# Separate value buffers refilled as soon as they are read, and one continuous sequence of row maxima

## The chip, the core and the metric

The kernel runs on one core of one Trainium2 chip. The metric is device time in microseconds (us). Five engines work side by side, each through its own instructions in a fixed order: PE (matrix products; its weight loads are listed as PEld), DVE (vector), ACT (activations), POOL (GpSimd) and SP, which here only issues DMAs. An instruction at the head of an engine's queue that waits holds up everything behind it.

## The reference

Attention over 8 batches and 8 heads, 1152 keys, 576 pooled queries, head size 64, followed by a gated unit:

```python
q_pool = q.reshape(B, H, S // factor, factor, D).mean(axis=3)
scores = scale * np.matmul(q_pool, k.transpose(0, 1, 3, 2))
scores = scores - np.max(scores, axis=-1, keepdims=True)
attn = np.exp(scores)
attn = attn / (np.sum(attn, axis=-1, keepdims=True) + 1e-09)
out = np.matmul(attn, v)                       # heads side by side: x, 8 x 576 x 512
h = np.maximum(x @ w_in, 0.0);  u, v = halves of h
v_n = normalised v;  v_s = w_spatial @ v_n + b_spatial
y = (u * v_s) @ w_out
```

## The kernel before

The work is cut into 32 pairs: two heads of one batch, four pairs to a batch. Every fp32 operand is split into a high and a low fp16 part (names ending in `hi`, `lo`) so that fp16 products give nearly fp32 accuracy. What happens to pair i, stage by stage:

- `load_kq(i)` fetches keys and queries into `kq` (one buffer, L222 and L223). `prep(i)` squares both for a scale (L132 on ACT), adds the two query rows that are pooled (L292 on POOL), splits into `xq`, `qhi`, `khi`, `klo` (L135, L302, L304 on ACT, L138 on DVE, L305 on POOL) and copies parts across partitions with DMAs (L299 to L313). There are three sets of these operands, so prep runs two pairs ahead.
- `norm_v(i)` fetches the values and squares them (L132) for a scale of the whole batch, four pairs ahead; `split_v(i)` fetches them again, scales and splits them into `vp` (L261, L262 on ACT, L264 on POOL), one pair ahead. Both fetch into `vt`, two buffers used in turn.
- `maxima(i)` finds the row maxima of the scores one pair ahead: 27 steps of a product of 384 columns (L342, or L333 for the mixed tile) into PSUM tile `pm` (or `pw` while no unit runs) and a reduction on DVE (L348). Then a last reduction `mx` (L352), a transpose (L356), a split into `mr` (L358, L359), and two small DMAs (L363) put the maxima into two extra rows of `xq`, so that the score product subtracts them.
- `attention(i)` has 18 score tiles: two products each (L506, L507) into one of three `pss` banks, the exponential on ACT (L512), every two tiles a split of the probabilities on POOL (L524), and four ticks later the products with the values (L428, L432, L435) into the single bank `o`; at the end of a head DVE normalises them into `xm` (L407, L408, L443). The 64 tail queries go the same way through `ptl` (L520, L524, L478 to L484).
- A unit of two batches (eight pairs) then runs as `gated_unit`, its steps mixed into the next eight pairs: DVE has much to do in the pairs 10, 18, 26 (normalising, L611 to L624) and 14, 22, 30 (a split, L138). The weights come as doubles and are turned into fp32 during the first eight pairs (`from_double`, L149 to L161, nearly all on DVE).

All of these are Python generators. `attention(i)` gives out 40 ticks, and after each tick the others advance by their rate (`Pace`: so many steps per tick, from a given tick on); at the end of a pair what is left is run out. That is the order of writing only. A scheduler beneath the language then sets the order on each engine: it goes by the order of writing, but where its own model of times holds an instruction not ready, it takes a later one that is. So an instruction may stand far ahead of where it was written, as far as its buffers allow; on the chip that order is fixed.

Of the kernel before, what the change touches and what calls it, by code (L numbers as in the profile page):

```python
# [12 lines left out]
F32 = mybir.dt.float32  # L13
# [18 lines left out]
def attn_sgu_kernel(ctx: ExitStack, tc: tile.TileContext, qT, kT, v, w_in, w_spT, b_sp, w_out, out):  # L32
    nc = tc.nc
    P = 128
    B, NHP, _, D, _, S = qT.shape
    NC = kT.shape[4]
    NP = B * NHP
# [20 lines left out]
    ld = ctx.enter_context(tc.tile_pool(name="ld", bufs=1))  # L58
# [66 lines left out]
    def scale_of(sq, name):  # L125
        tot = sm.tile([P, 1], F32, name=name + "t", bufs=2)
        nc.vector.reduce_sum(out=tot, in_=sq, axis=AX.X)
        yield
        return (yield from scales(tot, name))

    def square_sum(acc, src, junk):
        nc.scalar.activation(junk, src, AF.Square, bias=0.0, scale=1.0, accum_out=acc)  # L132
# [85 lines left out]
    def load_kq(i):  # L218

        b, hp = divmod(i, NHP)  # L220
        kq = ld.tile([P, 2 * KEYS], F32, name="kq")
        nc.sync.dma_start(out=kq[:, 0:KEYS], in_=kT[b, hp].rearrange("h d c p -> (h d) (c p)"))  # L222
        nc.sync.dma_start(out=kq[:, KEYS:], in_=qT[b, hp].rearrange("h d r s -> (h d) (r s)"))  # L223
        state[i] = {"kq": kq}

    def load_v(i):
        b, hp = divmod(i, NHP)
        vt = ld.tile([P, 2, NC, D], F32, name="vt", bufs=2)
        nc.sync.dma_start(
            out=vt.rearrange("p h c d -> p h (c d)"),  # L230
            in_=v[b, 2 * hp : 2 * hp + 2].rearrange("h (p c) d -> p h (c d)", c=NC),
        )
        return vt

    vsq = {}
    vscale = {}

    def norm_v(i):

        b, hp = divmod(i, NHP)  # L240
        if hp == 0:
            vsq[b] = sm.tile([P, 2 * NHP], F32, name="vsq", bufs=2)
        vt = load_v(i)
        yield
        yield
        for h in range(2):
            square_sum(vsq[b][:, 2 * hp + h : 2 * hp + h + 1], vt[:, h], vt[:, h])
            yield
        if hp == NHP - 1:
            vscale[b] = yield from scale_of(vsq.pop(b), "v")  # L250
            yield

    def split_v(i):

        vt = load_v(i)
        yield
        yield
        s_v = vscale[i // NHP][0]
        vp = vps[i % 2]
        for h in range(2):  # L260
            nc.scalar.activation(vt[:, h], vt[:, h], AF.Copy, bias=0.0, scale=s_v)  # L261
            nc.scalar.activation(vp[:, h, :, D : 2 * D], vt[:, h], AF.Copy, bias=0.0, scale=1.0)  # L262
            yield
            nc.gpsimd.tensor_sub(vp[:, h, :, 0:D], vt[:, h], vp[:, h, :, D : 2 * D])  # L264
            yield

    def values_ahead(i):
        if i + NHP < NP:
            yield from norm_v(i + NHP)
        if i + 1 < NP:  # L270
            yield from split_v(i + 1)

    def prep(i):
        st = state[i]
# [7 lines left out]
        for j in range(2):  # L282
            square_sum(sq[:, j : j + 1], kq[:, j * KEYS : (j + 1) * KEYS], KL[:, 0].rearrange("p c k -> p (c k)"))
            yield
        s, r = yield from scales(sq, "qk")
        esc = sm.tile([P, 1], F32, name="esc", bufs=NSET)
        nc.vector.scalar_tensor_tensor(
            out=esc, in0=r[:, 0:1], scalar=ESC, in1=r[:, 1:2], op0=ALU.mult, op1=ALU.mult
# [22 lines left out]
        nc.sync.dma_start(out=X[lower, 1], in_=X[upper, 0])  # L311
        nc.sync.dma_start(out=KL[lower, 1], in_=KL[upper, 0])
        nc.sync.dma_start(out=KL[D:KR, 0], in_=KL[D:KR, 1])  # L313
        yield


    def maxima(i):
        st = state[i]
# [52 lines left out]
    LAG = 4  # L371
    TAIL_SPLIT = 5
    TAIL_AT = 9
    PREP_AT = 3
    PREP_RATE = 0.35
    V_RATE = 0.35
    W_RATE = 0.25
    W_AT = 4
    MAX_RATE = 1.0

    units = []

# [6 lines left out]
    def ends_unit(i):  # L389
        return i % (2 * NHP) == 2 * NHP - 1  # L390
# [387 lines left out]
    def step(gen):  # L778
        return None if gen is None or next(gen, StopIteration) is StopIteration else gen
# [13 lines left out]
    def drain(gen):  # L793
        while gen is not None:
            gen = step(gen)

    load_kq(0)
    drain(norm_v(0))
    drain(prep(0))
    load_kq(1)  # L800
    for i in range(1, NHP):
        drain(norm_v(i))
    drain(maxima(0))
    drain(split_v(0))
    drain(prep(1))
    weights = load_weights()
    spatial_weights = [None]
    credit = 0.0
    for i in range(NP):
        if i + 2 < NP:  # L810
            load_kq(i + 2)
        run = [
            Pace(maxima(i + 1), MAX_RATE) if i + 1 < NP else None,
            Pace(values_ahead(i), V_RATE),
            Pace(prep(i + 2), PREP_RATE, PREP_AT) if i + 2 < NP else None,
            Pace(weights, W_RATE, W_AT if i == 0 else 0),
        ]
        for _ in attention(i):
            for r in run:
                if r:  # L820
                    r.tick()
            credit = min(credit + MOE_RATE, 2.0)
            while credit >= 1 and units:
                credit -= 1
                unit_step()
        for r in run[:3]:
            if r:
                drain(r.gen)
        weights = run[3].gen
        if ends_unit(i) and i < 2 * NHP:  # L830
            drain(weights)
            weights = None
            spatial_weights[0] = step(load_spatial())
# [49 lines left out]
```

## Time and profile before

| | |
|---|---|
| three runs | 1371.06, 1373.02, 1377.21 us; median 1373.02 |
| profiled execution | 1378.83 us, its span on the core 1377.1 us |
| granted PE clock, mean | 0.967 |
| busy share PE, DVE, ACT, POOL | 89%, 70%, 70%, 62% |
| DMA | 123.77 MB, mean 90 GB/s |
| chain that ended last | PE 47%, DVE 25%, ACT 8%, POOL 7%, DMA 7% |

In what follows a pair is taken to begin with the first of its 18 exponentials (L512). The first begins at 48.46 us, pair 8 at 328.6 us, the last pair (31) at 1236.7 us; what follows pair 31 is the last unit alone. A row of a group gives engine, line, tile names as out<-in and count, then busy us and mean ns of one, then the idle time of the engine just before and who ended it. A row of a wait gives who waited for whom, us in total, how often, and the longest. A row of a window gives its length, then busy us and count for each engine, the granted PE clock, the DMA share and GB/s.

### The profile page before, as it was taken

To read this page: it belongs to the slowest core of one execution; us is meant where nothing else is said; L and a number is where in the kernel's file an instruction comes from. 1 tells how busy PE (TensorE), PEld (TensorE's weight loads), DVE (VectorE), ACT (ScalarE), POOL (GpSimd) and SP (SyncE) were. 2 spreads that over 40 slices of the span, in tenths; PEclk is the share of its full clock that TensorE was granted. 3 is DMA by queue.
4 is the path that set the end of the run, shared out by engine and by line. 5 is a ranking of instruction groups with operands and counts; after the bars stand their busy time and mean duration, and the time that the engine had idled before them with its cause. 6 is when DMAs were issued, how large, how long until landed. Compare 5 with 4: busy or idle time off the path is not lost.

```text
span 1377.1 us, 33478 instructions
## 1 busy us (share of the span) xinstructions
PE 1222.1 (89%) x13696; PEld 741.5 (54%) x13696; DVE 967.1 (70%) x2068; ACT 970.6 (70%) x1632; POOL 847.0 (62%) x492
## 2 busy tenths in 40 slices
PE   3677887788998999889998999889998999899998
PEld 1354555555554665556555666555555566556443
DVE  5799889986869767765668766775667866761455
ACT  6777678779966777768776886768776776655333
POOL 3587677878755666657774766667666576655000
PEclk9998899989999999999999999999999999999999
DMA  7533343434333231244332132244331131101002
GB/s 252 166 97 109 94 124 94 128 93 139 113 96 96 79 94 56 62 126 135 96 96 87 51 91 84 74 118 135 104 96 42 47 94 55 28 24 40 8 1 69
DMA packets 56346, 123.77 MB, mean 90 GB/s; under 512 B 8256, under 2 KB 16448, under 8 KB 56192
## 3 DMA queue, kind: packets, MB, share of 16 engines
q1 hardware_dynamic: 56192, 121.63, 29.8%
q8 instruction: 107, 1.75, 0.5%
q14 instruction: 47, 0.39, 0.1%
HBM read 83.56 MB, written 9.44 MB: 68 GB/s over the span
## 4 chain that ended last, share of the span: by engine, by line
PE 47%; DVE 25%; ACT 8%; POOL 7%; DMA 7%; issue 4%; SPq 1%; POOLq 0%; ACTq 0%; DVEq 0%
DVE mt L348 7%; PE pss L507 5%; PE pss L506 5%; PE pw L688 5%; POOL pt L524 4%; PE pm L342 4%; PE pw L731 4%; PE pw L646 3%; PE o L435 3%; PE o L428 3%; PE pw L582 3%; ACT pt L512 3%; DMA kq<-in_qT_dram 3%; PE o L432 3%; DVE vv L138 2%
## 5 line engine op out<-in xcount | busy, mean ns | idle before, releaser
L524 POOL TENSOR_TENSOR pt<-pt 128x1024 f16<-128x1024 f32 x288 | 567.8, 1977 | 265.9 <-ACT pt L512 253.8
L512 ACT ACTIVATE pt<-pss,lnp,esc 128x512 f32<-128x512 f32 x576 | 439.4, 776 | 156.7 <-PE pss L507 148.1
L348 DVE TENSOR_REDUCE mt<-pm 128x1 f32<-128x384 f32 x730 | 395.8, 552 | 139.1 <-PE pm L342 119.2
L435 PE MATMUL o<-vp,pt 128*128 128x65 f16 x2304 | 282.8, 198 | 20.2 <-POOL pt L524 19.9
L428 PE MATMUL o<-vp,pt 128*128 128x65 f16 x2304 | 284.8, 196 | 13.0 <-DVE xm L443 12.8
L506 PE MATMUL pss<-qhi,khi 128*128 128x64 f16 (+1 forms) x1152 | 279.6, 294 | 9.1 <-ACT pt L512 8.0
L432 PE MATMUL o<-vp,pt 128*128 128x64 f16 x2304 | 284.5, 196 | 0.0
L507 PE MATMUL pss<-xq,klo 66*128 66x64 f16 (+1 forms) x1152 | 280.6, 295 | 4.1 <-DMA xq<-mr 4.1
L428 PEld LDWEIGHTS <-pt 128*128 128x128 bf16 x2304 | 222.7, 101 | 85.1 <-DVE xm L443 22.0
L432 PEld LDWEIGHTS <-pt 128*128 128x128 bf16 x2304 | 221.6, 100 | 50.7 <-issue 10.5
L342 PE MATMUL pm<-khi,qhi 128*128 128x384 f16 x652 | 217.9, 335 | 32.6 <-DVE mt L348 27.7
L435 PEld LDWEIGHTS <-pt 128*128 128x128 f16 x2304 | 220.7, 100 | 31.6 <-POOL pt L524 24.8
L507 PEld LDWEIGHTS <-klo 66*128 66x128 f16 x1152 | 99.1, 100 | 48.8 <-issue 17.3
L132 ACT ACTIVATE klo<-kq 128x1152 f16<-128x1152 f32 x64 | 74.6, 1166 | 63.7 <-DMA kq<-in_kT_dram 49.4
L506 PEld LDWEIGHTS <-khi 128*128 128x128 f16 x1152 | 103.5, 100 | 27.9 <-issue 12.2
L342 PEld LDWEIGHTS <-qhi 128*128 128x128 f16 x768 | 76.8, 101 | 66.3 <-issue 28.5
L524 POOL TENSOR_TENSOR ptl<-ptl 128x1152 f16<-128x1152 f32 x32 | 71.1, 2221 | 57.9 <-ACT ptl L520 57.9
L305 POOL TENSOR_TENSOR klo<-kq,khi 128x640 f16<-128x640 f32 x64 | 85.1, 1341 | 20.1 <-ACT khi L304 19.8
L520 ACT ACTIVATE ptl<-pss,lnp,esc 128x256 f32<-128x256 f32 (+1 forms) x128 | 75.6, 591 | 24.8 <-PE pss L507 24.2
L264 POOL TENSOR_TENSOR vp<-vt,vp 128x576 f16<-128x576 f32 x64 | 80.6, 1264 | 20.3 <-ACT vp L262 20.3
L582 PE MATMUL pw<-wi_h,xg 128*128 128x512 f16 x240 | 90.1, 382 | 0.0
L731 PE MATMUL pw<-wo_h,vv 128*128 128x512 f16 x216 | 80.3, 381 | 4.7 <-DVE vv L138 4.7
(177 smaller groups left out, 2394.2 us busy)
## 6 DMA issues: line engine op xcount, KB each, us to landing
vt<-in_v_dram SPq DMA_DIRECT2D x64, 576.0 KB
kq<-in_kT_dram SPq DMA_DIRECT2D x32, 576.0 KB
kq<-in_qT_dram SPq DMA_DIRECT2D x32, 576.0 KB
khi<-khi SPq DMA_DIRECT2D x96, 144.0 KB
out_dram<-row SPq DMA_DIRECT2D x24, 256.0 KB
qhi<-xq SPq DMA_DIRECT2D x64, 72.0 KB
klo<-klo SPq DMA_DIRECT2D x32, 144.0 KB
vv<-in_w_in_dram SPq DMA_DIRECT2D x8, 512.0 KB
```

Source lines behind the costliest of these rows:

```text
L305: nc.gpsimd.tensor_sub(KL[:, 0, a:z], k0[:, a:z], khh[:, 1, a:z])
L342: nc.tensor.matmul(pm[:, :W], lhsT=qhl[:, h, c0 : c0 + P], rhs=khh[:, h, n * NB : (n + 1) * NB, :], start=True, stop=True,)
L348: nc.vector.reduce_max(out=mt[:, t, n : n + 1], in_=pm[:, :W], axis=AX.X)
L428: nc.tensor.matmul(o[:, t], lhsT=top[:, cols], rhs=vp[:, D : D + D1], start=c == 0 and t == 0, stop=False, skip_group_check=True,)
L432: nc.tensor.matmul(o[:, t, 0:D], lhsT=top[:, cols], rhs=vp[:, 0:D], start=False, stop=False, skip_group_check=True)
L435: nc.tensor.matmul(o[:, t], lhsT=rst[:, cols], rhs=vp[:, D : D + D1], start=False, stop=c == NC - 1, skip_group_check=True,)
L506: nc.tensor.matmul(o, lhsT=khh[:, h, c, :], rhs=qhl[:, h, q], start=True, stop=False)
L507: nc.tensor.matmul(o, lhsT=KL[0:KR, h, c, :], rhs=X[0:KR, h, q], start=False, stop=True)
L512: nc.scalar.activation(pt, ps, AF.Exp, bias=lnp, scale=esc)
L524: nc.gpsimd.tensor_sub(t.bitcast(F16)[:, :, 0::2], t, t.bitcast(BF16)[:, :, 1::2])
L582: nc.tensor.matmul(ph, lhsT=xa[:, cc, c0 : c0 + P], rhs=wa[:, cc, DH:DF], start=n == 0, stop=n == 3 * NCC - 1,)
L731: nc.tensor.matmul(py, lhsT=ga[:, fc, c0 : c0 + P], rhs=wa[:, fc, :], start=m == 0, stop=m == end - 1)
```

## The change

Four things change.

1. The values get two buffers with names of their own: `vn` for `norm_v`, `vs` for `split_v` (one each, so the memory is the same). A fetch is written right behind the last read of its buffer: `norm_v(i)` ends with the fetch for the next one, `split_v(i)` with the fetch for `split_v(i + 1)`, and `prep(i)` ends with `load_kq(i + 1)`. Before, each was written where the data was wanted, with two idle steps behind it.
2. The maxima of the pairs 1 to 31 become one generator, `all_maxima`, which advances on all ticks at 0.85 steps per tick (before: one generator per pair, begun with pair i for pair i + 1, at 1.0). The maxima of a pair begin when those of the pair before are done and `prep` of the pair was finished at least four ticks ago (`LANDING`). What a pair must have is still run out before it.
3. `norm_v` and `split_v` are paced apart (0.4 from tick 0, and 0.3 from tick 16; before one after the other at 0.35), and `prep` begins at tick 2 in place of 3.
4. Before the first pair, `prep(0)` is written ahead of the four `norm_v`.

```diff
+    vts = {}
+    def load_v(i, name):
+        if i < NP:
+            b, hp = divmod(i, NHP)
+            vt = ld.tile([P, 2, NC, D], F32, name=name)
+            nc.sync.dma_start(...)
+            vts[i, name] = vt
...
-    def norm_v(i):
+    def norm_v(i, name="vn", ahead=1):
...
-        vt = load_v(i)
-        yield
-        yield
+        vt = vts.pop((i, name))
         for h in range(2):
             square_sum(vsq[b][:, 2 * hp + h : 2 * hp + h + 1], vt[:, h], vt[:, h])
             yield
+        load_v(i + ahead, name)
+        yield
...
     def split_v(i):
-        vt = load_v(i)
-        yield
-        yield
+        vt = vts.pop((i, "vs"))
...
             nc.gpsimd.tensor_sub(vp[:, h, :, 0:D], vt[:, h], vp[:, h, :, D : 2 * D])
             yield
-
-    def values_ahead(i):
-        if i + NHP < NP:
-            yield from norm_v(i + NHP)
-        if i + 1 < NP:
-            yield from split_v(i + 1)
+        load_v(i + 1, "vs")
+        yield
...
         nc.sync.dma_start(out=KL[D:KR, 0], in_=KL[D:KR, 1])
-        yield
-
+        if i + 1 < NP:
+            load_kq(i + 1)
+        prepped[i] = now[0] + LANDING
+        yield
+
+    prepped = {}
+    now = [0]
+    LANDING = 4
+    known = set()
+
+    def all_maxima():
+        for i in range(1, NP):
+            while prepped.get(i, 1 << 30) > now[0]:
+                yield
+            yield from maxima(i)
+            known.add(i)
...
-    PREP_AT = 3
+    PREP_AT = 2
     PREP_RATE = 0.35
-    V_RATE = 0.35
+    NORM_RATE = 0.4
+    V_RATE = 0.3
+    V_AT = 16
...
-    MAX_RATE = 1.0
+    MAX_RATE = 0.85
...
     load_kq(0)
-    drain(norm_v(0))
+    load_v(0, "vn")
+    load_v(1, "vs")
     drain(prep(0))
-    load_kq(1)
-    for i in range(1, NHP):
-        drain(norm_v(i))
+    drain(norm_v(0, "vn", 2))
+    drain(norm_v(1, "vs", 2))
+    drain(norm_v(2, "vn", 2))
+    drain(norm_v(3, "vs", -3))
     drain(maxima(0))
     drain(split_v(0))
     drain(prep(1))
     weights = load_weights()
+    maxima_pace = Pace(all_maxima(), MAX_RATE)
...
     for i in range(NP):
-        if i + 2 < NP:
-            load_kq(i + 2)
         run = [
-            Pace(maxima(i + 1), MAX_RATE) if i + 1 < NP else None,
-            Pace(values_ahead(i), V_RATE),
+            Pace(norm_v(i + NHP), NORM_RATE) if i + NHP < NP else None,
+            Pace(split_v(i + 1), V_RATE, V_AT) if i + 1 < NP else None,
             Pace(prep(i + 2), PREP_RATE, PREP_AT) if i + 2 < NP else None,
...
         for _ in attention(i):
-            for r in run:
+            now[0] += 1
+            for r in [maxima_pace, *run]:
...
         weights = run[3].gen
+        while i + 1 < NP and i + 1 not in known:
+            prepped[i + 1] = now[0]
+            maxima_pace.gen = step(maxima_pace.gen)
```

What the scheduler makes of it is seen on the engines. First DVE, from the end of pair 13 into pair 14, before the change (`mr` belongs to the maxima of pair 14, `row` and `u` to the unit; L348 are the first maxima of pair 15):

```order
L443 TENSOR_TENSOR xm<-o,den 128x4x64
L358 TENSOR_SCALAR mr<-pm 9x128
L359 SCALAR_TENSOR_TENSOR mr<-pm,mr 9x128
L695 SCALAR_TENSOR_TENSOR row<-pw,r_v,b_bc 128x512
L698 TENSOR_TENSOR u<-u,row 128x512
L695 SCALAR_TENSOR_TENSOR row<-pw,r_v,b_bc 128x64
L698 TENSOR_TENSOR u<-u,row 128x64
L635 TENSOR_SCALAR r_v<-wsr 128x1
L127 TENSOR_REDUCE gt<-gsq 128x1
L117 TENSOR_SCALAR gh<-pm 128x1
L121 TENSOR_SCALAR gs<-gh 128x1
L348 TENSOR_REDUCE mt<-pm 128x1
```

The same place with the change, where the lines have other numbers (L372 and L373 are L358 and L359, L459 is L443, L362 is L348, L711 and L714 are L695 and L698, L651 is L635):

```order
L373 SCALAR_TENSOR_TENSOR mr<-pm,mr 9x128
L459 TENSOR_TENSOR xm<-o,den 128x4x64
L362 TENSOR_REDUCE mt<-pm 128x1
L711 SCALAR_TENSOR_TENSOR row<-pw,r_v,b_bc 128x512
L362 TENSOR_REDUCE mt<-pm 128x1
L714 TENSOR_TENSOR u<-u,row 128x512
L362 TENSOR_REDUCE mt<-pm 128x1
L711 SCALAR_TENSOR_TENSOR row<-pw,r_v,b_bc 128x64
L362 TENSOR_REDUCE mt<-pm 128x1
L714 TENSOR_TENSOR u<-u,row 128x64
L362 TENSOR_REDUCE mt<-pm 128x1
L651 TENSOR_SCALAR r_v<-wsr 128x1
```

Five reductions of pair 15 now stand in the end of pair 13; before, none did, and the first came behind the start of the unit's split in pair 14. On PE the end of pair 13 (behind the transpose L356) holds five maxima products between the last score tiles, before none. So it is in the pairs 8 to 29, with five or six each, and in the pairs 1, 2 and 5; in the pairs 0, 3, 4, 6 and 7 the end of the pair still has none, or only its last moments.

Second SP, where the keys of pair 6 are fetched, before and then with the change (L222 and L223 fetch, `khi` and `klo` are the copies of prep; with the change L305, L306, L308 copy `khi`, L310 and L311 `klo`, L233 fetches values):

```order
L308 DMA khi_118<-khi_118 64x1152
L312 DMA klo_109<-klo_109 64x1152
L222 DMA kq<-in_kT_dram 128x1152
L363 DMA xq_114<-mr 1x9x128 x2
L310 DMA khi_118<-khi_118 64x1152
L313 DMA klo_109<-klo_109 2x1152
L223 DMA kq<-in_qT_dram 128x1152
```

```order
L306 DMA khi_118<-khi_118 64x1152
L310 DMA klo_109<-klo_109 64x1152
L222 DMA kq<-in_kT_dram 128x1152
L308 DMA khi_118<-khi_118 64x1152
L311 DMA klo_109<-klo_109 2x1152
L223 DMA kq<-in_qT_dram 128x1152
```

The fetch of keys and queries stands at the same place, behind the first copy of `klo`: it was there although it was written elsewhere. The DMAs of the maxima (L363) are no longer among these, here.

Third SP about the fetch for pair 12, before and then with the change (L299 and L297 begin the copies of the next prep):

```order
L313 DMA klo_109<-klo_109 2x1152
L223 DMA kq<-in_qT_dram 128x1152
L229 DMA vt<-in_v_dram 128x2x576
L363 DMA xq_114<-mr 1x9x128 x2
L229 DMA vt<-in_v_dram 128x2x576 x2
L299 DMA qhi_119<-xq_113 64x576
```

```order
L311 DMA klo_109<-klo_109 2x1152
L223 DMA kq<-in_qT_dram 128x1152
L233 DMA vn<-in_v_dram 128x2x576
L377 DMA xq_114<-mr 1x9x128 x2
L233 DMA vn<-in_v_dram 128x2x576 x3
L233 DMA vs<-in_v_dram 128x2x576
L297 DMA qhi_119<-xq_113 64x576
```

Three fetches into the one buffer `vn` stand in a row ahead of the next copies. With a buffer of its own the chain of `norm_v` runs ahead of its place: all its squares stand before pair 14, where before nearly every pair up to 25 had one.

More of the change, by code (lines that the diff above doesn't have):

```diff
@@ L224, in load_kq @@
         state[i] = {"kq": kq}
[L226 to L233, printed above, removed]
+    vts = {}
[3 more added lines that the diff above has]
+            vt = ld.tile([P, 2, NC, D], F32, name=name)
+            nc.sync.dma_start(
+                out=vt.rearrange("p h c d -> p h (c d)"),
+                in_=v[b, 2 * hp : 2 * hp + 2].rearrange("h (p c) d -> p h (c d)", c=NC),
+            )
+            vts[i, name] = vt
     vsq = {}
     vscale = {}
-    def norm_v(i):
+    def norm_v(i, name="vn", ahead=1):
         b, hp = divmod(i, NHP)
```

## The prediction

> **What bounds the kernel now.** I read first the span by stretch, cut where the exponentials of a pair begin: the start; pairs 0 to 7; pairs 8 to 30; pair 31 and the last unit.
>
> ```profile
> core 0: us, PE busy (x) PEld busy (x) DVE busy (x) ACT busy (x) POOL busy (x), PEclk, DMA share, GB/s
> 0.00:48.46 48.46, 16.31 (x51) 5.90 (x52) 27.96 (x65) 30.91 (x61) 17.12 (x22) 1.00 0.71 226
> 48.46:328.60 280.14, 224.58 (x2803) 147.37 (x2803) 246.49 (x457) 215.74 (x364) 214.55 (x118) 0.90 0.37 109
> 328.60:1236.70 908.10, 845.85 (x9811) 518.13 (x9809) 636.05 (x1413) 667.27 (x1111) 594.85 (x343) 0.98 0.29 86
> 1236.70:1377.10 140.40, 135.33 (x1037) 70.05 (x1035) 56.64 (x134) 56.73 (x98) 20.49 (x11) 1.00 0.09 31
> ```
>
> PE is idle for 48.46 - 16.31 = 32.2 us at the start, 280.14 - 224.58 = 55.6 in pairs 0 to 7, 62.3 in pairs 8 to 30 and 5.1 at the end. The eight early pairs are DVE's: it is busy for 246.49 of 280.14 us, so its idle time, 33.7 us, is all that a better order could take from them. The next 23 pairs are PE's, at 93% busy. The change leaves the end alone.
>
> Then the waits, for what PE waits on:
>
> ```profile
> ACT klo L132 <- DMA kq<-in_kT_dram: 49.4, 20, 4.7
> PE pm L342 <- DVE mt L348: 27.7, 35, 2.2
> PE o L435 <- POOL pt L524: 19.9, 24, 2.3
> PE pm L356 <- DVE mx L352: 13.4, 9, 3.7
> PE o L428 <- DVE xm L443: 12.8, 11, 2.5
> PE pw L342 <- DMA khi<-khi: 10.4, 1, 10.4
> ```
>
> Most of what holds PE up after the start is DVE being late with a small result (27.7 + 13.4 + 12.8), and some is POOL late with a split (19.9). ACT's 49.4 us on the keys is the largest wait for a fetch.
>
> Last, where inside a pair the time lies: pair 3 in two pieces, the second part of pair 13 in two, pairs 14 and 18 in two each; the second piece is always the last three to six score tiles.
>
> ```profile
> 152.60:176.00 23.40, 19.72 (x237) 13.07 (x236) 22.26 (x43) 18.13 (x31) 16.18 (x9) 0.85 0.14 43
> 176.00:189.20 13.20, 10.10 (x134) 6.35 (x131) 9.13 (x19) 9.25 (x17) 10.88 (x7) 0.87 0.68 185
> 545.50:559.90 14.40, 13.98 (x174) 8.72 (x171) 10.82 (x27) 9.56 (x18) 8.75 (x6) 1.00 0.59 171
> 559.90:568.60 8.70, 7.61 (x103) 4.49 (x100) 4.78 (x10) 6.09 (x12) 8.70 (x6) 1.00 0.01 3
> 568.60:599.00 30.40, 23.56 (x283) 15.00 (x283) 28.08 (x48) 22.68 (x38) 18.64 (x11) 1.00 0.16 44
> 599.00:609.50 10.50, 9.67 (x106) 5.25 (x102) 3.93 (x13) 5.82 (x9) 3.90 (x3) 1.00 0.66 180
> 722.30:759.10 36.80, 31.82 (x327) 19.09 (x325) 32.03 (x76) 23.02 (x39) 19.09 (x11) 0.91 0.30 90
> 759.10:768.70 9.60, 8.86 (x111) 5.14 (x108) 9.11 (x14) 8.71 (x16) 5.99 (x4) 1.00 0.01 2
> ```
>
> In pair 3 DVE works 22.26 of 23.40 us and then only 9.13 of 13.20. In pair 13 the end belongs to POOL, 8.70 of 8.70 us, with DVE at 4.78 and PE idle for 1.09. In pair 14 DVE holds PE up (28.08 of 30.40 busy, PE idle 6.84) and then has nothing to do (3.93 of 10.50). The ends of the pairs are where DVE has room: no maxima stand there.
>
> **The change part by part.** *Fetches of keys and queries: 0.* The order on SP has them where they were, behind the first copy of `klo`, so the 49.4 us of ACT stay; that wait hides behind products that PE still has in store.
>
> ```profile
> 666.31 0.58 SPq L222 DMA_DIRECT2D kq<-in_kT_dram  x1
> 671.90 1.16 ACT L132 ACTIVATE klo<-kq 128x1152 f16<-128x1152 f32 x1 [3.53 <-DMA kq<-in_kT_dram]
> 676.30 1.40 POOL L292 TENSOR_TENSOR kq<-kq 128x576 f32<-128x576 f32 x1 [5.89 <-ACT klo L132]
> ```
>
> Here, in pair 16, ACT loses 3.53 us and POOL 5.89. Were PE's store gone, each such pair could cost those 3.5 us. `prep` starts one tick of 40 earlier, about 1 us of a pair, and no wait hangs on it: 0.
>
> *The start: -2.* Before, ACT waits for the values of pair 1 ahead of prep's splits; with the change the splits (L135, L302, L304) stand ahead of that work.
>
> ```profile
> 39.12 1.44 ACT L261 ACTIVATE vt<-vt,vs 128x576 f32<-128x576 f32 x2 [4.46 <-DMA vt<-in_v_dram]
> 41.61 0.76 ACT L135 ACTIVATE xq<-kq,qks 128x576 f16<-128x576 f32 x1
> 47.83 0.72 ACT L157 ACTIVATE vv<-vv,bias_e 128x512 int32<-128x512 int32 x1 [0.52 <-DVE vv L155]
> ```
>
> At best the 4.46 us go. But the first exponential stands behind L157, which comes at the end of a chain of weight work between DVE and ACT, so at worst nothing goes. I take about half.
>
> *The maxima: one reduction, one product.*
>
> ```profile
> L348 DVE TENSOR_REDUCE mt<-pm 128x1 f32<-128x384 f32 x730 | 395.8, 552 | 139.1 <-PE pm L342 119.2 <-PE pm L333 12.1 <-PE pss L506 0.4
> L348 DVE TENSOR_REDUCE mt<-pm x730: 520/557/560, 30.4 to 1228.4; 128x1 f32<-128x384 f32 x183
> L161 DVE TENSOR_TENSOR u<-u,vv x12: 673/1631/2375, 18.3 to 297.7; 128x512 f32<-128x512 f32 x12
> 188.34 0.33 PE L342 MATMUL pw<-khi,qhi 128*128 128x384 f16 x1
> 188.51 0.32 PE L342 MATMUL pm<-khi,qhi 128*128 128x384 f16 x1
> ```
>
> A reduction holds DVE for 0.552 us, a product holds PE for 0.17 us (188.51 - 188.34). None is added or removed; five or six a pair go from the body of a pair to the end of the one before. The second and third row give minimum, median and maximum in ns: the reduction, which reads PSUM, never takes more than 0.560 us, wherever POOL is busy, while L161, which reads two tiles from SBUF, takes up to 3.5 times its least. So the ends of the pairs, where POOL is busiest, are no dearer for reductions. The Trainium skill's page "SBUF — State Buffer", section "Who interferes with whom", says that on this chip reductions never contend with GpSimd for the port that it shares with the vector engine, and that an instruction with two SBUF inputs does. By that rule the trace agrees; by the other answer, with the reductions of L161's kind, six would take 6 x 1.63 = 9.8 us, more than the whole of pair 13's end.
>
> *Pairs 0 to 7: -8.* Three of the eight (1, 2 and 5) now have maxima at the end. Six reductions are 6 x 0.552 = 3.3 us, which DVE's idle 13.20 - 9.13 = 4.07 us hold, and DVE is the bound in the body, so up to 3.3 each, 10 us; I count 8. Bounds: 0, if the body then waits for something else, and 33.7, all of DVE's idle time.
>
> *The quiet pairs of 8 to 30: -9.* There are 16 (9 to 29 without 10, 14, 18, 22 and 26). The end lasts as long as POOL needs; six products, 1.0 us, fit into PE's 1.09 idle there, and the body, where PE works 13.98 of 14.40, is shorter by as much: at best 16 x 1.0 = 16, at worst 0. I take 0.55 of a pair, as ends like that of pair 14 have less room.
>
> *Pairs 14, 22, 30: -4.* Five reductions leave the stretch where DVE holds PE up: 5 x 0.552 = 2.8 us, three times 8.3 at best, 0 at worst; half. In the pairs 10, 18 and 26 DVE is full to the end (9.11 of 9.60), and as many reductions come in there as go out: 0.
>
> *New waits: +5.* PE stands still where a maximum at the end of a pair finds its copies not landed. The copies' queue:
>
> ```profile
> SPq L229 <- POOL vp L264: 257.2, 25, 25.9
> SPq L363 <- DVE mr L359: 169.7, 30, 10.0
> SPq L312 <- POOL klo L305: 27.7, 23, 1.9
> 663.72 0.46 SPq L307 DMA_DIRECT2D khi<-khi  x1
> ```
>
> In pair 16 the copies of `khi` are issued from 663.72 us on, and its end begins some 14 us later: no wait. In early pairs they come later, and the longest wait for them in the trace is 10.4 us, at the start. Between 0 and two such waits, 20; I take 5, near 0, since most pairs are like 16.
>
> **Sum:** -2 - 8 - 9 - 4 + 5 = -18. The profiled execution takes 1378.83 us (span 1377.1 and 1.7 around it), so 1361 for a profiled one; it lies 5.8 above the median of the three runs, 1373.02, from which the same sum gives 1373 - 18 = **1355 us**.
>
> **The rivals.** *Slower: the values' chain heads SP's queue.* In the pairs 10 to 14 up to three fetches into `vn` stand ahead of the next prep's copies, each waiting for ACT to read the last one.
>
> ```profile
> 35.01 4.02 DMA vt<-in_v_dram
> 45.88 0.67 ACT L132 ACTIVATE vt<-vt 128x576 f32<-128x576 f32 x1
> 46.46 0.19 ACT L132 ACTIVATION_READ_ACCUMULATOR vt<-vt 128x1 f32 x1
> ```
>
> One round is a fetch of 4.0 us and two squares of 0.86, so 5.7; three are 17 us, and the copies of pair 16 have 14 to spare. It decides from there on: past it prep, the keys' fetch and the maxima at the end are all late, and PE waits for the remainder, 3 us, and for the keys, 3.5: 6.5 in each of five pairs, 32 us. Then 1373 - 18 + 32 = 1387. Against it: the order was made with those fetches in view, and SP now waits 257 us for POOL without harm.
>
> *No change:* the gains at the ends need the body to be bound by what was moved. If POOL's splits (19.9 us of PE's waits) and ACT's exponentials take its place, only the start and the early pairs give anything, and the new waits take it: -2 - 4 + 5 = -1, so 1372.
>
> *More: the clock.* The granted clock is 0.90 in pairs 0 to 7 and 0.98 in 8 to 30: 0.10 x 280 = 28 us and 0.02 x 908 = 18 lost to it. If steadier work brings back a third, 15 us, the time is 1340. The Trainium skill's page "TensorE: Matmul & The Clock Gate", Part 1, has the clock halved after one idle window of about 3.4 us. The trace agrees only in part: between 152.60 and 176.00 PE is idle for 3.68 us in all, in several pieces, and still has 0.85. So by the rule nothing would change here but at one wait (3.7 us, the longest on `mx`), by the rows more could.
>
> **How the numbers follow.** The forecast has a chance of 0.52, the clock 0.14, no change 0.20, slower 0.14. A change under 0.5% (7 us) can hardly be told from none here, where three runs spread over 6 us; so faster means under 1366, slower over 1380. Faster: 0.52 and 0.14, less a few hundredths that end within 0.5%, is 0.64; the same 0.22; slower 0.14. The range: down, the early pairs at 20 in place of 8, the quiet at 14 and no new waits give 1355 - 12 - 5 - 5 = 1333, rounded up to 1335; up, it takes in no change and ends at 1379, short of the slower case. The forecast's own range is 1343 to 1365.
>
> **What would show it.** The early pairs' stretch below 275 us with DVE above 89%; PE idle in pairs 8 to 30 below 50 us; the wait of L342's successor for reductions below 20 us; a first exponential at about 46 us. Wrong would be: PE waits for `khi` copies in many pairs; SP issuing the copies of prep behind `vn` fetches after the tenth tile of pairs 10 to 14; or a stretch of pairs 8 to 30 that is no shorter with PE's waits on POOL grown.

## The result, and the profile after

The changed kernel takes **1395.17 us** (four runs, 1394.0 to 1396.71), the kernel before 1372.04 beside it (1369.9 to 1377.21): ratio 1.0164, 95% interval 1.0133 to 1.0195. It is 23 us slower where 18 less were forecast, and lies above the range. The profiled execution took 1396.71 us, its span 1394.9, that is 17.8 more than the span before. The windows below come from one execution of each kernel. Executions of the kernel before spread over 10 us (1367.28 to 1377.51 in 18 further runs), and its profiled one, 1378.83, was a long one, so a difference of a few us in one stretch is not shown to be the change's.

The windows, cut as before at the first exponential of pairs 0, 8 and 31 (L528 is the former L512), the columns as in the prediction:

```profile
0.00:46.43 46.43, 16.46 (x51) 5.80 (x52) 28.79 (x65) 31.15 (x61) 15.73 (x21) 1.00 0.72 235
46.43:321.14 274.71, 217.34 (x2776) 144.19 (x2776) 242.04 (x453) 215.77 (x362) 215.10 (x120) 0.92 0.37 111
321.14:1254.62 933.48, 852.93 (x9839) 527.41 (x9837) 643.53 (x1416) 668.57 (x1113) 594.73 (x343) 0.98 0.29 84
1254.62:1394.93 140.31, 135.29 (x1037) 70.07 (x1035) 56.49 (x134) 56.67 (x98) 20.47 (x11) 1.00 0.09 31
```

The start is 2.1 us shorter, the early pairs 5.4. Pairs 8 to 30 take 933.5 us in place of 908.1: **the loss, 25.3 us, is there**. PE's idle time in them is 933.48 - 852.93 = 80.6 us, before 62.3: 18.3 of the 25.3. The rest, 7.0, is PE's own busy time.

Its waits, the rows that answer to those of the prediction:

```profile
ACT klo L132 <- DMA kq<-in_kT_dram: 46.8, 16, 4.8
PE pm L356 <- DVE mt L362: 44.9, 47, 5.1
PE o L451 <- POOL pt L540: 17.1, 17, 2.8
PE o L444 <- DVE xm L459: 13.5, 13, 2.4
PE pm L356 <- DVE xg L418: 10.4, 6, 3.8
PEld pm L112 <- DVE mt L362: 9.1, 9, 2.8
PE pw L356 <- DMA qhi<-qhi: 9.7, 1, 9.7
```

PE's wait of a maxima product for a reduction (L356 for L362, formerly L342 for L348) grew from 27.7 to 44.9 us. In pairs 8 to 30 alone, where the loss is, the rows of PE's waits for a reduction are these, first before, then after (L112 is a product for a scale, L333 and L347 are those of the mixed tile, L479 is one of the tail queries):

```profile
PE pm L342 <- DVE mt L348: 20.1, 23, 2.2
PE pm L333 <- DVE mt L348: 1.5, 2, 0.8
PE pm L112 <- DVE mt L348: 0.8, 3, 0.3
```
```profile
PE pm L356 <- DVE mt L362: 34.4, 37, 3.4
PE pm L112 <- DVE mt L362: 6.5, 3, 2.5
PE pm L347 <- DVE mt L362: 2.1, 3, 0.7
PE pm L479 <- DVE mt L362: 0.9, 2, 0.4
```

They add up to 22.4 us before and 43.9 after: 21.5 more, where PE's idle time there grew by 18.3. So what PE waits longer for is DVE's reductions, in the pairs 10, 18 and 26 above all (11.5 us before, 23.0 after). No wait for the `khi` copies stands in the list; the one wait for prep's copies, 9.7 us, is at the start, as the 10.4 before.

By pairs, from the same cuts (us, sums over the pairs named):

| | before | after | difference | predicted |
|---|---|---|---|---|
| start | 48.5 | 46.4 | -2.1 | -2 |
| pairs 0 to 7 | 280.1 | 274.7 | -5.4 | -8 |
| pair 8 | 34.6 | 38.4 | +3.8 | |
| 10, 18, 26 | 138.0 | 149.1 | +11.1 | 0 |
| 14, 22, 30 | 119.1 | 108.7 | -10.4 | -4 |
| the 16 quiet pairs | 616.6 | 637.4 | +20.8 | -9 |
| pair 31 and the last unit | 140.3 | 140.3 | 0 | |

Pair 13 in the two pieces of the prediction, cut at the same exponentials:

```profile
551.36:566.33 14.97, 14.54 (x180) 9.13 (x179) 10.07 (x26) 10.35 (x19) 10.58 (x7) 1.00 0.48 131
566.33:574.18 7.85, 7.22 (x99) 4.47 (x98) 5.05 (x10) 5.59 (x12) 7.85 (x6) 1.00 0.01 3
```

The moved maxima are there: the end holds five of their products, before none. It is no longer for them (7.85 us against 8.70). But the piece ahead is not shorter either (14.97 against 14.40).

### The profile page after: what moved, and what is told of

The parts are those of the page before. It is cut to its first block, busy times and chain, and to the rows that moved or that the text cites. A ratio compares the mean times of both kernels' runs of the same rounds, so it can differ in the third digit from the quotient of the medians.

```text
span 1394.9 us, 33501 instructions
## 1 busy us (share of the span) xinstructions
PE 1222.0 (88%) x13696; PEld 747.5 (54%) x13696; DVE 970.9 (70%) x2068; ACT 972.2 (70%) x1632; POOL 846.0 (61%) x492
## 3 DMA queue, kind: packets, MB, share of 16 engines
q8 instruction: 107, 1.75, 0.5%
## 4 chain that ended last, share of the span: by engine, by line
PE 45%; DVE 30%; ACT 9%; DMA 6%; POOL 5%; issue 4%; SPq 0%; POOLq 0%; ACTq 0%; DVEq 0%
DVE mt L362 10%; PE pss L522 5%; PE pss L523 5%; PE pm L356 4%; PE pw L747 4%; PE pw L704 4%; PE pw L598 3%; POOL pt L540 3%; ACT pt L528 3%; PE pw L662 3%; PE o L451 3%; PE o L444 2%; PE o L448 2%; DVE vv L138 2%; DMA kq<-in_kT_dram 2%
## 5 line engine op out<-in xcount | busy, mean ns | idle before, releaser
L528 ACT ACTIVATE pt<-pss,lnp,esc 128x512 f32<-128x512 f32 x576 | 440.1, 777 | 167.4 <-PE pss L523 157.6
L362 DVE TENSOR_REDUCE mt<-pm 128x1 f32<-128x384 f32 x728 | 395.7, 551 | 180.2 <-PE pm L356 169.6
L444 PE MATMUL o<-vp,pt 128*128 128x65 f16 x2304 | 279.7, 195 | 13.6 <-DVE xm L459 13.5
L451 PE MATMUL o<-vp,pt 128*128 128x65 f16 x2304 | 276.2, 197 | 17.4 <-POOL pt L540 17.1
L448 PE MATMUL o<-vp,pt 128*128 128x64 f16 x2304 | 279.0, 195 | 0.0
L356 PE MATMUL pm<-khi,qhi 128*128 128x384 f16 x654 | 219.5, 336 | 62.4 <-DVE mt L362 44.9
L132 ACT ACTIVATE klo<-kq 128x1152 f16<-128x1152 f32 x64 | 74.3, 1160 | 57.9 <-DMA kq<-in_kT_dram 46.8
L356 PEld LDWEIGHTS <-qhi 128*128 128x128 f16 x768 | 76.9, 102 | 58.1 <-issue 16.5
L266 POOL TENSOR_TENSOR vp<-vs,vp 128x576 f16<-128x576 f32 x64 | 82.8, 1294 | 10.9 <-ACT vp L264 10.9
L662 PE MATMUL pw<-xg,wi_h 128*128 128x512 f16 (+1 forms) x336 | 82.5, 335 | 3.3 <-ACT u L672 3.3
```

The lines of the kernel that those rows point to most:

```text
L356: nc.tensor.matmul(pm[:, :W], lhsT=qhl[:, h, c0 : c0 + P], rhs=khh[:, h, n * NB : (n + 1) * NB, :], start=True, stop=True,)
L362: nc.vector.reduce_max(out=mt[:, t, n : n + 1], in_=pm[:, :W], axis=AX.X)
L444: nc.tensor.matmul(o[:, t], lhsT=top[:, cols], rhs=vp[:, D : D + D1], start=c == 0 and t == 0, stop=False, skip_group_check=True,)
L448: nc.tensor.matmul(o[:, t, 0:D], lhsT=top[:, cols], rhs=vp[:, 0:D], start=False, stop=False, skip_group_check=True)
L451: nc.tensor.matmul(o[:, t], lhsT=rst[:, cols], rhs=vp[:, D : D + D1], start=False, stop=c == NC - 1, skip_group_check=True,)
L528: nc.scalar.activation(pt, ps, AF.Exp, bias=lnp, scale=esc)
```

## The experiments

**1. The change in parts.** The theories: A, the maxima at the ends of pairs cost; B, the values' chain of fetches; C, the rate of 0.85. The first kernel (called "the fetches alone") has the change's buffers, fetches, paces and prep tick, with the maxima one pair at a time at 1.0; the second is the kernel before with `all_maxima`; the third and fourth are the changed kernel with one edit.

```diff
 e1: -    maxima_pace = Pace(all_maxima(), MAX_RATE)          # after, but
     +            Pace(maxima(i + 1), MAX_RATE), with MAX_RATE = 1.0
 e2: +    maxima_pace = Pace(all_maxima(), 0.85)              # before, but
 e3: -    MAX_RATE = 0.85                                     # after, but
     +    MAX_RATE = 1.0
 e4: -            while prepped.get(i, 1 << 30) > now[0]:
     +            while prepped.get(i, 1 << 30) > now[0] or (i - 1) not in begun:
```

> The change with the maxima as they were: one generator per pair, begun with the pair before, 1.0 steps per tick. The new value buffers, the refills behind the last read and the paces of norm_v, split_v and prep stay. Theory A (the 25 us that pairs 8 to 30 lost come from maxima standing at the ends of pairs): no loss is left, 1362 to 1372 us, since the gain at the start (2 us) stays. Rival B (they come from the values' chain running ahead and the new order on ACT and SP): 1385 to 1398. Rival C (from the rate 0.85, which spreads the maxima over more ticks): as A.

> The kernel before with the one sequence of maxima alone (0.85 steps per tick, from four ticks past prep); value buffers, fetches and paces as before. Theory A: the whole loss, 1388 to 1400 us, with PE's waits on reductions in pairs 8 to 30 about 1.7 times those of before. Rival B: 1365 to 1375. Rival C: as A.

> The change with 1.0 maxima steps per tick in place of 0.85; they still begin at the end of the pair before. Theory A: the loss stays, 1385 to 1400 us. Rival C: it goes, 1360 to 1374. Rival B: stays.

> The change with 0.85 kept, but a pair's maxima do not begin before the pair ahead of it does, so none stand at the end of the pair before. Theory A: the loss goes, 1362 to 1378 us (the last maxima come late in the pair, which may cost a few us by their DMAs). Rival C: it stays, 1385 to 1400. Rival B: it stays.

Measured against the kernel before at 1372.15 us: fetches alone 1408.93, ratio 1.0263 (1.0242 to 1.0284); maxima alone 1391.96, 1.0142 (1.011 to 1.0174); rate 1.0: 1394.07, 1.0172 (1.0127 to 1.0216); no shift 1415.6, 1.031 (1.0278 to 1.0341). The fetches alone cost 37 us, the maxima alone 20, both together 23. A falls by the first (its range for the second, 1388 to 1400, came true), B by the second, and the first lies above B's range too; C falls by the third. The fourth is no clean test of A, for its edit takes away only half of the shift: between the last reduction `mx` of a pair and the next pair's first exponential, DVE still has 2 to 5 reductions in the pairs 8 to 29 (5 to 7 with the change, 0 to 2 before), and in pairs 0 to 7 even 11 to 14 (0 to 13 with the change). Its pairs 8 to 30 take 939.0 us, and 16 of the 20 us that it loses to the changed kernel are in pairs 0 to 7. Costs that don't add up pointed to something that each edit disturbs.

**2. Edits that do nothing.** In the kernel before one constant is moved; no work, buffer or fetch changes. The fourth kernel has the change in pairs 0 to 7 only, with the maxima at 1.0.

```diff
 n1: -    V_RATE = 0.35      n2: -    PREP_AT = 3     n3: -    MAX_RATE = 1.0
     +    V_RATE = 0.36          +    PREP_AT = 2         +    MAX_RATE = 0.97
 h1:      for i in range(NP):                                 # after, but
     +        if i < EARLY: run = [...]    # EARLY = 8: the change's paces and fetches
     +        else: load_kq(i + 2); run = [Pace(maxima(i + 1), 1.0), Pace(values_ahead(i), 0.35),
     +                                     Pace(prep(i + 2), PREP_RATE, 3), Pace(weights, W_RATE)]
```

> The kernel before with one pace moved by 3%: V_RATE 0.36 in place of 0.35. No work, buffer, fetch or wait is changed; 172 of PE's 26,874 rows stand more than ten places from where they stood. Theory D (what costs is not any part of the change but the order that the scheduler deals anew, of which the kernel before had a good one): little is dealt anew, 1368 to 1390. Theory S (a particular part of the change costs: the values' fetches, or the maxima): 1367 to 1377.

> The kernel before with prep begun at tick 2 in place of 3, one of the constants of the change and the one that the prediction costed at 0. 1,755 of PE's rows move by more than ten places, about as many as in the kernel with the fetches alone (1,923), which took 1409. Theory D: 1382 to 1405, pairs 8 to 30 longer by 10 us or more, with PE's waits for reductions and DVE's stretched operations up. Theory S: 1367 to 1377.

> The kernel before with MAX_RATE 0.97 in place of 1.0: the maxima of each pair are spread over one tick more, nothing else. 2,730 of PE's rows move by more than ten places. Theory D: 1382 to 1405. Theory S: 1367 to 1377.

> The change in pairs 0 to 7 alone (its fetches, paces and run of maxima, these at 1.0), and from pair 8 on the fetches, paces and maxima of the kernel before. The start gives 2.5 us and the early pairs 6 to 13 (as measured with the fetches and with the rate of 1.0). Theory S: pairs 8 to 30 are as before (908 us), so 1356 to 1366. Theory D: the state in which the scheduler comes to pair 8 is another, so the order from there is dealt anew too, and 8 to 30 take 915 to 945: 1366 to 1396.

Before was 1372.78 here. The values' pace: 1384.25, ratio 1.01 (1.0068 to 1.0132). Prep's tick: **1397.48, 1.0196** (1.0165 to 1.0228). The maxima's pace: 1377.08, 1.0039 (1.0022 to 1.0056). The early change: 1368.38, 0.997 (0.995 to 0.9991). D held for the first two: a pace moved by 3% costs 11 us, and one tick, which the prediction costed at 0, costs 25, as much as the change. For the maxima's pace it missed: 1377.08 lies below D's 1382 and at the edge of S's 1377, although more rows moved there (2,730) than with the tick (1,755). So how many rows move doesn't tell the cost. The fourth is in D's range and outside S's, with pairs 8 to 30 at 914.0 us, between the two. With the tick pairs 8 to 30 take 934.2 us with 80.5 idle on PE; the changed kernel's take 933.5 with 80.6. S expected 1367 to 1377 for each of the three constants.

**3. Is that tick the cause in the change?** Theory P says so.

```diff
 p1, p2, p3: -    PREP_AT = 2        # in after, in e1, in e3
             +    PREP_AT = 3
 n4:         -    PREP_AT = 3        # in before
             +    PREP_AT = 4
```

> The kernel with the change, prep begun at tick 3 as before. Theory P (prep one tick earlier is what costs: alone it lengthened pairs 8 to 30 by 26 us, to 934.2, and the change has 933.5): pairs 8 to 30 come back to 908 to 916, PE no longer waits for a reduction ahead of the product of L112 nor 3.6 us for xm, 1366 to 1378. Theory D (any order dealt anew costs, P's tick was one such deal): 8 to 30 stay at 920 to 945, 1378 to 1405.

> The change's buffers, refills and paces of the values, maxima one pair at a time as before, and prep at tick 3: what was 1409 with prep at tick 2. Theory P: 908 to 918 in pairs 8 to 30 and the early gain of 13 kept, 1358 to 1372. Theory D: 920 to 960, 1375 to 1405. A third, F (the values' fetches cost by themselves in pairs 13, 21 and 29, where the fetches alone lost 5 us each): these three stay at 130 where they were 117, 1378 to 1395.

> The change with the maxima at 1.0 and prep at tick 3: only the fetches, the paces of the values and the one run of maxima are left of it. Theory P: as the change with prep at 3, 1362 to 1378, less in the early pairs. Theory D: 1375 to 1405, and apart from the change with prep at 3 by 5 us or more either way, since 13,299 rows against 9,932 stand otherwise than before.

> The kernel before with prep at tick 4, the other way from the change. 1,022 of PE's rows move by more than ten places. Theory P (earlier is worse): no loss, 1366 to 1376. Theory D: a loss here too, 1378 to 1398.

Before was 1371.53. The change with tick 3: 1389.94, ratio 1.0141 (1.0113 to 1.017); the fetches with it 1387.63, 1.0118 (1.0094 to 1.0141); rate 1.0 with it 1386.73, 1.0111 (1.009 to 1.0132); the kernel before with tick 4 1395.31, 1.0178 (1.0148 to 1.0208). P explains a part: 21 of the 37 us of the fetches alone, 5 of the change's 23. But the other way costs as much: of the three ticks tried the tuned one is best, and both its neighbours cost 24 to 25 us. D's ranges for the time hold in all four; but the third kernel lay 3 us from the first, not 5 or more as D had it. F, on the values' fetches, held in time but not in place: the pairs 13, 21 and 29 take 122.1 us, between F's 130 and the 117 before. The kernel before with one constant moved, four times, has a mean of 1388.5; the changed kernel and its variants of rate and tick (e3, p1, p3) lie at 1387 to 1395. So the change can't be told from such neighbours of the kernel before (1377 to 1397), while it loses 23 us against the one good order. That is a comparison of four kernels with four, not a proof that the parts of the change cost nothing: other variants of it, the fetches alone and e4, are slower than all of these (1409 and 1416).

PE's waits for reductions in pairs 8 to 30, 22.4 us before and 43.9 with the change, are 43.7 with the maxima alone, but also 49.0 with prep at tick 4, where the maxima are left one pair at a time.

**4. Is the loss local?** With the tick at 2 the pairs 10, 18 and 26 take 149.3 us, with 3 they take 138.0.

```diff
 m1: -    Pace(prep(i + 2), PREP_RATE, PREP_AT)               # before, but
     +    Pace(prep(i + 2), PREP_RATE, PREP_AT if i % 8 == 2 else 2)
 m3: +    Pace(prep(i + 2), PREP_RATE, 2 if i % 8 == 2 else PREP_AT)
 m2: +            if i % 8 == 5: carried = Pace(maxima_and_next(i + 1), 1.0)    # h1, but
     +            elif i % 8 == 6: carried.rate = 0.85
```

> The kernel before with prep at tick 2 in all pairs but 2, 10, 18 and 26, which keep tick 3. In pair 18 PE's order is then row for row that of the kernel before (with tick 2 everywhere the product of L112 stood eighteen rows earlier there, with a wait of 2.8 us for a reduction, and a product of L428 waited 3.5 us for xm). Theory L (the loss is local: certain rows of certain pairs): the three pairs take 137 to 140 us (before 138.0, tick 2 everywhere 149.3), pairs 8 to 30 920 to 926, the time 1381 to 1390. Theory W (any order but the tuned one loses as a whole): the three pairs take what they like, 143 to 152, and 8 to 30 928 to 945.

> The other half of the first: prep at tick 2 in pairs 2, 10, 18 and 26 alone. In pair 18 the rows stand as with tick 2 everywhere. Theory L: the three pairs take 147 to 151 us, the other pairs from 8 on as before (770), so 8 to 30 917 to 922 and the time 1379 to 1387. Theory W: 8 to 30 anywhere from 908 to 940, the three pairs not apart from the rest.

> The change in pairs 0 to 7 (as in the run before of that kind, 1368), and from pair 8 on the kernel before but for one thing: in pairs 13, 21 and 29 the maxima of 14, 22 and 30 are followed at once by those of the next pair, and in 14, 22 and 30 the rest runs at 0.85. In the change these three pairs took 108.7 us against 119.1. Theory L: they take 108 to 114, the others stay within 3 us, 1358 to 1366. Theory W: what is gained there is lost elsewhere, 1366 to 1385.

Before was 1371.46. All but the three pairs: 1391.93, ratio 1.0147 (1.0124 to 1.017), the three pairs 137.6 us, 8 to 30 925.1. The three pairs alone: 1385.48, 1.0103 (1.0083 to 1.0122), the three 147.7, the rest from 8 on 766.2 (before 770.2). L held for the pairs: they follow their own tick, not that of the others. In time the first ended 2 us above L's bound, and pairs 8 to 30 of the second took 913.9 us, 3 below it (its profiled execution, 1378.22 us, was the shortest of the five, 7 below their median). The three pairs are 11 of the 26 us that the tick costs there. In the first kernel the 16 quiet pairs still take 639.1 us in place of 616.6; which of their rows cost this stays open. The windows of pair 18, before, with tick 2 everywhere, everywhere but there, and there alone:

```profile
722.29:768.74 46.45, 40.74 (x433) 24.26 (x432) 41.18 (x89) 31.77 (x55) 25.12 (x14) 0.93 0.24 72
```
```profile
718.81:768.99 50.18, 41.19 (x432) 24.82 (x431) 43.18 (x89) 32.21 (x56) 26.56 (x15) 0.90 0.22 66
```
```profile
722.47:768.99 46.52, 40.73 (x433) 24.13 (x432) 41.42 (x89) 31.73 (x56) 25.13 (x14) 0.93 0.25 72
```
```profile
716.38:765.01 48.63, 38.78 (x432) 23.45 (x430) 43.39 (x89) 32.19 (x56) 26.55 (x15) 0.96 0.23 68
```

DVE's busy time in the pair, 41.2 and 41.4 with tick 3 and 43.2 and 43.4 with tick 2, is of the same 89 instructions: something stretches them.

m2 was to keep what gained: 1366.43 us, ratio **0.9963 (0.995 to 0.9977)**, faster than both kernels by a little, and 0.4 above L's range, in W's. Its start and early pairs take 46.2 and 264.7 us, and 14, 22 and 30 take 111.3 (118.2 without m2's edit); pair 13 lost 4.2 of it again, and 8, 11 and 12 together are 6.7 longer than before. Its pairs 8 to 30 take 911.6 us against 908.2: as W had it, what 14, 22 and 30 gain is lost elsewhere, and the gain that is left comes from the start and the early pairs.

**5. What makes a row cost.** A piece of pair 18 with tick 2, in order of time (start, duration, in brackets idle time before it and its end):

```profile
755.83 1.73 POOL L292 TENSOR_TENSOR kq<-kq 128x576 f32<-128x576 f32 x1 [0.70 <-ACT klo L132]
756.22 3.65 DVE L618 TENSOR_SCALAR row<-vv,mv,rs 128x512 f32<-128x512 f32 x2
757.52 2.07 POOL L524 TENSOR_TENSOR pt<-pt 128x1024 f16<-128x1024 f32 x1
760.19 0.42 DVE L443 TENSOR_TENSOR xm<-o,den 128x256 f32<-128x256 f32 x1
760.67 0.24 PE L428 MATMUL o<-vp,pt 128*128 128x65 f16 x1 [3.54 <-DVE xm L443]
762.24 0.53 DVE L618 TENSOR_SCALAR row<-vv,mv,rs 128x512 f32<-128x512 f32 x1
```

Two operations L618 take 3.65 us, and the second ends 0.28 us after POOL's second; alone, 2.4 us later, one takes 0.53. Behind them in DVE's order stands `xm`, and PE's products with the values wait 3.54 us for it. In the kernel before POOL's L292 stands one place later there. In the same pair of the changed kernel:

```profile
749.10 2.08 POOL L540 TENSOR_TENSOR pt<-pt 128x1024 f16<-128x1024 f32 x1
749.35 2.11 DVE L634 TENSOR_SCALAR row<-vv,mv,rs 128x512 f32<-128x512 f32 x1
751.38 0.55 DVE L362 TENSOR_REDUCE mt<-pm 128x1 f32<-128x384 f32 x1
751.98 0.32 PE L356 MATMUL pm<-khi,qhi 128*128 128x384 f16 x1 [1.21 <-DVE mt L362]
752.93 1.90 POOL L540 TENSOR_TENSOR pt<-pt 128x1024 f16<-128x1024 f32 x1 [0.46 <-ACT pt L528]
753.05 2.05 DVE L634 TENSOR_SCALAR row<-vv,mv,rs 128x512 f32<-128x512 f32 x1
755.62 0.32 PE L356 MATMUL pm<-khi,qhi 128*128 128x384 f16 x1 [2.31 <-DVE mt L362]
```

The reduction itself is as short as ever (0.55), as the prediction had it; but it stands behind an operation that is held, and PE waits 1.21 and 2.31 us. Even a tiny operation is held until 0.03 us after POOL's end, here one of nine elements a partition in the kernel before (minimum, median, maximum in ns):

```profile
L613 DVE TENSOR_SCALAR sd<-sd x16: 161/173/1754, 411.5 to 1301.9; 128x9 f32<-128x9 f32 x16
```

The Trainium skill's page "SBUF — State Buffer", section "Who interferes with whom", says that `tensor_scalar` can enter a mode that takes the pair of ports shared with GpSimd, and that whoever comes first has it for the whole instruction while the other is blocked. These rows agree. In the traces of the kernel before, the changed one and the one with tick 2, 28 of the 108 operations L618 or L634 take 1.18 to 2.42 us, and each of these ends 0.28 to 0.29 us after a POOL instruction that it ran beside; the others take 0.50 to 0.69.

This is a part of the waits, not all. While PE waited for reductions in pairs 8 to 30, DVE was in operations of over 1 us for 9.5 us before and 19.7 after, and in reductions themselves for 12.5 and 22.9.

Three kernels without POOL's largest work, the split of the main probabilities, test it. They leave out the low part of these probabilities: the third product of a value tile takes the high part once more.

```diff
 q1, q2, q3: -        rst = pt.bitcast(F16)[:, k % 2, 0::2]      # in before, after, n2
             +        rst = top
             -            if k % 2 == 1:
             -                split(st["pt"][-1])
```

> The kernel before without POOL's split of the main probabilities (L524 for pt, 568 of POOL's 946 us): the low part is left out and the third product of each value tile takes the high part once more, so PE's work is the same. Theory H (vector operations held until a POOL operation ends are what makes PE wait): DVE's busy time in pairs 8 to 30 falls from 636 to 560 to 595 us, PE's idle time there from 62 to under 42, and 8 to 30 take under 885 us. Theory R (the places of the rows alone): DVE's busy time falls too, but PE's idle time stays at 55 to 80, and 8 to 30 take 895 to 935; the waits on POOL itself, 5.8 us, go in either case.

> The changed kernel without POOL's split of the main probabilities, as in the one before. Theory H: the loss of 25 us in pairs 8 to 30 shrinks to under 10, PE's idle time there falls from 81 to under 45. Theory R: it stays 15 to 35 us longer than the first of the three there.

> The kernel before with prep at tick 2, again without that split. Theory H: the loss of 26 us in pairs 8 to 30 shrinks to under 10, and 10, 18 and 26 together to within 4 us of the first of the three. Theory R: 15 to 35 us longer there, the three pairs 8 us or more.

(POOL is busy for 847 us in the trace of the kernel before, not the 946 of the first expectation.) Measured: 1268.69 us, ratio 0.9248 (0.9221 to 0.9274), for the kernel before; 1281.15, 0.934 (0.9307 to 0.9373), for the changed one; 1277.47, 0.9313 (0.9282 to 0.9344), with the tick. Their pairs 8 to 30, in this order:

```profile
275.09:1127.63 852.54, 828.41 (x9806) 512.12 (x9803) 577.55 (x1412) 667.31 (x1114) 195.41 (x135) 1.00 0.32 92
```
```profile
267.06:1139.33 872.27, 833.34 (x9817) 517.13 (x9816) 585.01 (x1416) 664.68 (x1115) 197.13 (x135) 1.00 0.31 90
```
```profile
275.71:1134.75 859.04, 830.43 (x9780) 512.25 (x9777) 581.43 (x1409) 664.75 (x1111) 198.46 (x135) 1.00 0.31 90
```

DVE's busy time falls from 636 to 578 us with the same 1412 instructions (1413 before), PE's idle time from 62.3 to 24.1, the clock is 1.00. Of PE's 38.2 us less, 5.8 are direct waits for the split; the wait of a maxima product for a reduction falls from 20.1 to 2.4. So far H. The tick's loss in these pairs falls from 26.0 to 6.5 us, and the three pairs differ by 3.1 (118.3 against 115.2): H again. But **the change's loss there stays at 19.7 of 25.3**: R, for the change, although PE's idle time falls below H's 45, to 38.9, with 14.8 of it in waits for reductions in place of 2.4. In the pairs 10, 18 and 26 the change still costs 7.3 us of 11.1, in the quiet pairs 14.1 of 20.8, and in the time of the whole kernel 12.5 us of 23 (1281.15 against 1268.69). One caution: without the split the scheduler deals each of the three orders anew, so part of each of these differences may come from the new order.

## Why the prediction was wrong

**The frame: the step that failed.** It took the order of pairs 8 to 30 as given and priced only what was moved, each reduction at its own 0.552 us. The order there is dealt by the scheduler from all that is written, and the kernel before had a good one: four moves of one constant (n1 to n4) cost 4 to 25 us. In the order of the changed kernel reductions come later for PE: its waits for them in pairs 8 to 30 grew from 22.4 to 43.9 us, where the prediction looked for less (27.7 in the whole kernel, to fall below 20; it became 44.9). PE's idle time there, to fall below 50 us, became 80.6. Which edit of the change makes them late is not settled.

**Keys and queries, "0": right; prep one tick earlier, "0": wrong.** ACT's wait is 46.8 us (49.4). The tick alone took pairs 8 to 30 from 908 to 934 us; that this nearly equals the change's 933.5 is chance, since taking the tick out of the change gives back 5 us of 23. "No wait hangs on it" looked for a wait on prep; what came, in pair 18, was prep's product L112 and POOL's L292 at other places in their engines' orders, ahead of what others needed.

**The start, -2: right**, -2.1; first exponential at 46.43 us, "about 46".

**Pairs 0 to 7, -8: right sign**, -5.4, within the bounds. DVE is busy for 242.04 of 274.71 us, 88%; "above 89%" failed narrowly. The reason given isn't borne out: the maxima alone left these pairs at 280.2 us, while prep's tick alone brought 269.0 and the fetches alone 266.8, both without the one sequence of maxima. The sign was luck.

**The quiet pairs, -9: wrong, +20.8.** That six products fit into the end was right (pair 13's end is not longer), and so was the price of the reductions. That the body gets shorter by what leaves it was wrong: in pair 13 it did not. In the 16 pairs together PE is idle for 37.1 us in place of 25.5, of which waits for reductions are 9.2 in place of 2.4, and it is busy for 9.2 more; why it is busy for longer stays open.

**14, 22, 30, -4: right sign**, -10.4, above the best case of 8.3. m2 has it too, 7 us by one edit, and the maxima alone 5; but so has prep's tick alone, 6 us without a maximum moved, so the reason given explains a part at most.

**10, 18, 26, 0: wrong, +11.1.** "As many come in as go out" counted the reductions. What they stand behind was left out: PE waits there for reductions queued behind other work of DVE, 23.0 us in place of 11.5; operations of over 1 us take 13.7 us of this, before 5.7. What POOL holds is so a part of the cause and not the whole: without POOL's split 7.3 of the 11.1 us stay. The maxima alone, without the fetches or the tick, take these three pairs to 151.4 us, and the tick alone to 149.3. The row on L161 (673 to 2375 ns) was quoted to show that reductions are not stretched; that a reduction queued behind such an operation is late was not priced.

**New waits, +5: wrong in kind.** PE waited for no copies of `khi`. The sum of the spans is -2.1 - 5.4 + 3.8 + 11.1 - 10.4 + 20.8 = +17.8.

**The rivals.** The values' chain was there: up to four fetches into `vn` stand together in SP's order in pair 10.

```profile
442.46 19.01 SPq L233 DMA_DIRECT2D vn<-in_v_dram  x4
462.92 0.54 SPq L297 DMA_DIRECT2D qhi<-xq  x1
```

Prep's copies follow it, 1.5 us after, and PE waits for none of them; its price of 32 us was not paid, and maxima without any of the fetches lose 20. Its time, 1387, was nearer than the forecast, by luck: the mechanism was another. "No change" had POOL's splits take the place of what was moved; PE's waits for them fell, from 19.9 to 17.1 us, and the time rose. The clock did not recover by the change: 0.972 against 0.967.

## What to carry to other kernels

Where a scheduler sets each engine's order, the kernel that lies before you may sit in a good order, and an edit can draw another. So time some edits without content first (here +4 to +25 us): a change has to be read against that spread, and tried where it gained alone (here the start and the early pairs, 0.3 to 0.4% in h1 and m2). Before pricing a step at nothing, look at what it will stand ahead of in each engine's order, and price a short operation by what is queued in front of it.

## What the runs showed of the hardware that was not expected

Leaving out POOL's split of the probabilities gains far more than PE's waits for it: 19.9 us in the list of waits, but 102 us of the kernel's time (1371.05 to 1268.69), part of which may come from the new order. Beside it `tensor_scalar` operations of 0.16 and 0.53 us last until just after POOL's instruction ends, 1.75 and some 2 us. PE's granted clock rose too: in pairs 0 to 7 it is 0.98 in place of 0.90 when the split is left out and PE's idle time there falls from 55.6 to 25.0 us (226.82 - 201.85), as the row below shows. The sum of the idle time doesn't set it alone, for with the change it is 0.92 at 57.4 us idle. In the trace of the kernel before the granted clock drops to 0.5 eighteen times, each time right behind a stretch of 3.4 us in which PE was idle for 1.4 to 2.9 us, so no stretch without any product was needed.

```profile
48.27:275.09 226.82, 201.85 (x2810) 135.29 (x2810) 194.35 (x458) 212.06 (x363) 69.31 (x46) 0.98 0.44 132
```

What stays open is how much of the change's 20 us that remain without the split belongs to the maxima at the ends of the pairs, and how much to that kernel's own deal.
